# An S5 plus SwiGLU kernel: the start-up loads are shared out anew between two queues, and the first products go by halves of the contraction

## The chip, the cores and the metric

The kernel runs on one core of a Trainium2 chip. The metric is the device time of one execution in microseconds. Before the change the median of three runs is 212.19 us (211.9 to 212.24).

## The reference

The input x is 2048 rows of 512 numbers (bfloat16). Each row is normalised, and the result is the sum of x, a state-space branch and a gated feed-forward branch on the normalised rows:

```
x  = A_x
xn = _layernorm(x, axis=-1)

# state-space branch (512 complex states)
dt = exp(log_dt);  Lam_bar = exp(dt * Lam)
B_bar = ((Lam_bar - 1.0) / Lam)[:, None] * Bmat
Bu = einsum("bld,pd->blp", xn, B_bar)
h  = Lam_bar * h + Bu[:, t, :]          # for each t
y  = 2.0 * einsum("blp,dp->bld", hseq, Cmat).real + xn * Dskip

# gated branch, F = 1792
gate = xn @ w1;  up = xn @ w3
out  = (silu(gate) * up) @ w2

return x + y + out
```

## The kernel before

The 2048 rows are cut into four blocks of 512 (`TBLK`), and each block into four chunks of 128 rows (`CPB`). The 512 input features are four contraction tiles of 128 (`NDT`), the 1792 hidden features are 14 tiles `f` (`NFT`). Products want the normalised rows transposed, with features on the partitions: `xnT` of a block holds that. For blocks 1 to 3 a DMA does the transposing, off the start. For block 0 TensorE does it, chunk by chunk, since nothing else can run yet.

The order of every engine's instructions is the order in which the program writes them (`manual_schedule`); work of VectorE and ScalarE that is to lie under products waits in a queue of tasks which `drain` empties at a given rate. A transfer is issued by SP or by ScalarE, each in its own order. Transfers take completion semaphores in turn out of eight, so a transfer that gets a semaphore still in use waits, on its issuing engine, until the earlier transfer that holds it has landed.

The start, which the change touches, runs as follows.

- **Loads.** SP issues rows 0 to 127 of x (line 79), rows 128 to 255 (line 80), then by `load_w13(0, 4, 2)` (line 115) the first four tiles of w1 and w3, each as two halves of the contraction (tiles 0 and 1, then 2 and 3; 256 KB a half), then the next tiles, block 1 of x, the remaining w1 and w3, and so on. ScalarE issues a load of the first parameter vector (line 111), rows 256 to 511 (line 112) and the two other parameter vectors (lines 113 and 114).
- **Warm-up.** `keep_warm` (line 147) lets TensorE multiply constants while nothing is there: eight matmuls of 512 columns and five of 128, and two more of 128 columns between the transposes of chunk 0 and of chunk 1. Their results are never read.
- **Normalising.** `stats`, `aggr` and `normed` run on VectorE, `rstd_act` on ScalarE, chunk after chunk. `turn` transposes a chunk on TensorE into PSUM, a half (two tiles) at a time for chunks 0 and 1; `put` copies it into `xnT`, on ScalarE for chunks 0 and 1, on VectorE for 2 and 3.
- **First products.** `begun` is three pairs of PSUM banks, for the gate and the up product of f 0, 1 and 2. Their products start before the whole block is normalised: `ahead(w_sbs, fs, c, n, dts, joins)` multiplies for the tiles `fs` the chunks c to c + n with the contraction tiles `dts`. Chunk 1 is transposed by way of the banks of f 2, so that products of f 2 must wait until it has been copied out. The order (lines 516 to 551): transposes of chunk 0, of chunk 1 (both halves), the w1 products of f 0 to 2 with contraction tiles 0 and 1 for chunk 0, for chunk 1, then tiles 2 and 3 for both chunks at once, then w3, then chunk 2, a transpose of the parameters (line 544), and so on.
- **After the start** `glu_up(0)` goes on from f 0 to 13 with all four chunks, `ssm_in` makes the inputs of the scan, VectorE runs the scan, and `y_out` multiplies by w2 and by C and writes a chunk.

The parameters' transpose feeds `par_cols` (ScalarE, GpSimd), then r_col (line 549) and the load of ScalarE's table for silu (line 550).

Of the kernel before, what the change touches and what calls it, by code (L numbers as in the profile page):

```python
# [16 lines left out]
P = 128  # L17
# [3 lines left out]
def kernel(  # L21
# [24 lines left out]
    nc = tc.nc  # L46
# [8 lines left out]
    NDT = D // P  # L55
# [20 lines left out]
    def load_rows(c0, c1, eng):  # L76
        eng.dma_start(out=x_blk[0][:, c0:c1, :], in_=xv[:, 0, c0:c1, :])  # L77

    load_rows(0, 1, nc.sync)
    load_rows(1, 2, nc.sync)  # L80
    nc.scalar.preload_act_table_set("natural_log_exp_and_others")
    w1_sb = const.tile([P, NDT, F], BF16, name="w1_sb")
    w3_sb = const.tile([P, NDT, F], BF16, name="w3_sb")
    w2_sb = const.tile([P, NFT, D], BF16, name="w2_sb")
    w1v = B_w1.rearrange("(t p) f -> p t f", p=P)
    w3v = B_w3.rearrange("(t p) f -> p t f", p=P)

    H = NDT // 2

    def load_w13(f0, f1, parts=1):  # L90
        fs = slice(f0 * P, f1 * P)
        for w_sb, wv in ((w1_sb, w1v), (w3_sb, w3v)):
            for i in range(parts):
                ds = slice(i * NDT // parts, (i + 1) * NDT // parts)
                nc.sync.dma_start(out=w_sb[:, ds, fs], in_=wv[:, ds, fs])

    dskip_row = const.tile([P, D], BF16, name="dskip_row")
    bt = [const.tile([P, NDT, PS], BF16, name=f"bt{ri}") for ri in range(2)]
# [9 lines left out]
    def load_prm(i, src, eng):  # L108
        eng.dma_start(out=prm[i * NPT:(i + 1) * NPT, :], in_=src.rearrange("(t p) -> t p", p=P))

    load_prm(0, A_Lambda_re, nc.scalar)
    load_rows(2, CPB, nc.scalar)
    load_prm(1, A_Lambda_im, nc.scalar)
    load_prm(2, A_log_dt, nc.scalar)
    load_w13(0, 4, 2)
    load_w13(4, 8)
    nc.sync.dma_start(out=x_blk[1], in_=xv[:, 1, :, :])
    load_w13(8, NFT)
    nc.sync.dma_start(out=dskip_row, in_=A_Dskip.partition_broadcast(P))
    load_turned(bt[0], A_B_re)  # L120
# [26 lines left out]
    def keep_warm(n, width=512):  # L147
        one = nc.const_aps.tensor_like(1.0, like=ident[:, 0:1])
        for _ in range(n):
            nc.tensor.matmul(out=begun[0][0][:, :width], lhsT=one.to_broadcast([P, P]), rhs=one.to_broadcast([P, width]),  # L150
                             start=True, stop=True)

    keep_warm(8)
    keep_warm(5, P)


    mv_all = const.tile([P, NBLK * CPB, 2], FP32, name="mv_all")
# [4 lines left out]
    def stats(c):  # L162
        sums[c] = work.tile([P, 6], FP32, name="stats", bufs=4)
        nc.vector.bn_stats(out=sums[c], in_=x_blk[c // CPB][:, c % CPB, :])  # L164
# [4 lines left out]
    def rstd_act(c0, c1):  # L169
        y = rstd_all[:, c0:c1]  # L170
        nc.scalar.activation(out=y, in_=mv_all[:, c0:c1, 1], func=ACT.Ln, bias=LN_EPS)
        nc.scalar.activation(out=y, in_=y, func=ACT.Exp, scale=-0.5)
# [15 lines left out]
    def normed(c, parts=1):  # L188
        xn = work.tile([P, D], BF16, name="xn", bufs=8)
        for i in range(parts):  # L190
            ds = slice(i * D // parts, (i + 1) * D // parts)
            nc.vector.tensor_scalar(out=xn[:, ds], in0=x_blk[c // CPB][:, c % CPB, ds], scalar1=mv_all[:, c, 0:1],
                                    scalar2=rstd_all[:, c:c + 1], op0=ALU.subtract, op1=ALU.mult)
        return xn
# [54 lines left out]
    def turn(c, pxt, d0=0, d1=NDT):  # L249
        for dt in range(d0, d1):  # L250
            nc.tensor.transpose(out=pxt[:, dt - d0, :], in_=xn0[c][:, dt * P:(dt + 1) * P], identity=ident)  # L251

    def put(c, pxt, eng, d0=0, d1=NDT):
        dst = xnTs[0][:, d0:d1, c * P:(c + 1) * P]
        if eng is nc.scalar:
            nc.scalar.activation(out=dst, in_=pxt, func=ACT.Copy)
        else:
            nc.vector.tensor_copy(out=dst, in_=pxt)
# [110 lines left out]
    def glu_mm(b, f, w_sb, ps, ts, dts=range(NDT), joins=False):  # L369

        for dt in dts:
            nc.tensor.matmul(out=ps[:, ts], lhsT=w_sb[:, dt, f * P:(f + 1) * P], rhs=xnTs[b][:, dt, ts],  # L372
                             start=(dt == 0 and not joins), stop=(dt == NDT - 1))
# [128 lines left out]
    def ahead(w_sbs, fs, c, n=1, dts=range(NDT), joins=False):  # L502
        for f in fs:
            for w_sb in w_sbs:
                glu_mm(0, f, w_sb, begun[f][w_sb is w3_sb], slice(c * P, (c + n) * P), dts, joins)
# [13 lines left out]
    xn0[1] = normed(1, 2)  # L519
    turn(0, tb, H, NDT)  # L520
    put(0, tb, nc.scalar, H, NDT)
    keep_warm(2, P)
    turn(1, t1[0], 0, H)
    put(1, t1[0], nc.scalar, 0, H)
    turn(1, t1[1], H, NDT)
    put(1, t1[1], nc.scalar, H, NDT)
    stats(2)
    aggr(2)
    rstd_act(2, 3)
    stats(3)  # L530
    B3 = (0, 1, 2)
    lo, hi = range(H), range(H, NDT)
    ahead((w1_sb,), B3, 0, 1, lo)
    ahead((w1_sb,), B3, 1, 1, lo, True)
    ahead((w1_sb,), B3, 0, 2, hi)
    xn0[2] = normed(2)
    aggr(3)
    rstd_act(3, 4)
    ahead((w3_sb,), B3, 0, 2, lo)
    turn(2, t2)  # L540
    put(2, t2, nc.vector)
    xn0[3] = normed(3)
    ahead((w3_sb,), B3, 0, 2, hi)
    nc.tensor.transpose(out=pprm, in_=prm, identity=ident)  # L544
# [63 lines left out]
```

## Time and profile before

| | |
|---|---|
| median of three runs | 212.19 us |
| profiled execution | 212.11 us |
| its span (first to last instruction) | 210.3 us |
| TensorE (PE) busy | 206.6 us, 98% of the span |
| VectorE (DVE) busy | 173.5 us, 82% |
| ScalarE (ACT) busy | 93.4 us, 44% |
| GpSimd (POOL) busy | 6.0 us, 3% |

The span is counted from the program's first instruction to its last; 1.8 us of the execution's time lie around it. All moments in the text are microseconds from the start of the span. In a profile line `L372` is line 372 of the kernel printed above, `PE` is TensorE's multiplying, `PEld` its weight loads, `SPq` and `ACTq` the issue of transfers on SP and ScalarE. A line of the timeline has the start, the time from the first of its instructions to the end of the last, the engine, the line, the operation with the tiles written and read, their shapes and the number of instructions; in brackets is how long the engine stood idle before it and what it waited for. Matmuls overlap, so that their rate is the distance between two starts and not the time of one.

The largest groups by busy time are all products: those of w1 (58.2 us), of w3 (58.4), of w2 (51.2), of C (30.4) and of B (28.1).

### The profile page before, as it was taken

The page shows a single profiled execution, that of the slowest core. Times are in us where ns is not written, and L with a number is a line of the kernel's source. Part 1 is how long each engine was busy: PE and PEld are TensorE (multiplying, and loading weights), DVE is VectorE, ACT ScalarE, POOL GpSimd, SP SyncE. Part 2 cuts the span into 40 slices and gives each one's busy share as a digit, 9 for nine tenths or more (in the row PEclk, how much of TensorE's full clock was granted, in tenths as well). Part 3 has the DMA queues.
Part 4 walks back from the last instruction along what each step waited for, and adds up shares of the span by engine and source line. Part 5 has one row for each costly group of instructions (what it writes and reads, how often), then busy time and mean ns, then how long its engine had stood idle before and what let it go on. Part 6 is the DMA issues. An engine that isn't in the chain of part 4 may idle for free.

```text
span 210.3 us, 2878 instructions
## 1 busy us (share of the span) xinstructions
PE 206.6 (98%) x1036; PEld 97.7 (46%) x1036; DVE 173.5 (82%) x346; ACT 93.4 (44%) x167; POOL 6.0 (3%) x27
## 2 busy tenths in 40 slices
PE   8999999999999999999999999999999999999994
PEld 3864444444444444444444444444444444444453
DVE  4699989989999999999999999999999999121111
ACT  3599967666666200066666600036666620000000
POOL 2010320000000000000000000000000000000000
PEclk9999999999999999999999999999999999999999
DMA  5999599944000000000004200100000000000110
GB/s 165 294 366 219 109 178 325 217 106 100 0 3 0 0 25 25 28 26 0 0 0 77 28 1 24 50 25 5 0 0 0 0 3 25 27 25 25 34 44 25
DMA packets 25014, 13.69 MB, mean 65 GB/s; under 512 B 15912, under 2 KB 25000, under 8 KB 25000
## 3 DMA queue, kind: packets, MB, share of 16 engines
q1 hardware_dynamic: 24704, 13.24, 26.1%
q10 hardware_dynamic: 296, 0.27, 0.4%
q8 instruction: 8, 0.13, 0.3%
q14 instruction: 6, 0.05, 0.1%
HBM read 7.74 MB, written 2.10 MB: 47 GB/s over the span
## 4 chain that ended last, share of the span: by engine, by line
PE 96%; DMA 2%; SPq 0%; DVE 0%; issue 0%
PE g_ps L372 23%; PE u_ps L372 23%; PE y_ps L488 23%; PE y_ps L493 13%; PE bu_ps L411 13%; DMA w_sb<-in_B_w_dram 2%; SPq L77 0%; PE xt_ps L251 0%; DVE o L498 0%; PE xt_ps L544 0%
## 5 line engine op out<-in xcount | busy, mean ns | idle before, releaser
L372 PEld LDWEIGHTS <-w_sb 128*128 128x128 bf16 x502 | 46.4, 98 | 50.6 <-DMA w_sb<-in_B_w_dram 0.6
L372 PE MATMUL g_ps<-xnT,w_sb 128*128 128x512 bf16 (+2 forms) x254 | 58.2, 354 | 0.3 <-DMA w_sb<-in_B_w_dram 0.3
L372 PE MATMUL u_ps<-xnT,w_sb 128*128 128x512 bf16 (+2 forms) x248 | 58.4, 358 | 0.0
L488 PE MATMUL y_ps<-w_sb,hgT 128*128 128x512 bf16 (+2 forms) x238 | 51.2, 366 | 0.0
L390 ACT ACTIVATE up<-u_ps 128x512 bf16<-128x512 f32 x56 | 34.0, 607 | 14.9 <-PE u_ps L372 14.9
L413 ACT ACTIVATE u<-bu_ps 128x512 bf16<-128x512 f32 x32 | 19.1, 597 | 46.3 <-PE bu_ps L411 46.3
L388 ACT ACTIVATE sl<-g_ps 128x512 bf16<-128x512 f32 x56 | 34.0, 608 | 9.9 <-PE g_ps L372 9.2
L445 DVE TENSOR_TENSOR_SCAN ab<-r_col,h,ab 128x256 bf16<-128x256 f32 x56 | 37.7, 733 | 0.2
L488 PEld LDWEIGHTS <-hgT 128*128 128x128 bf16 x238 | 22.8, 98 | 25.9
L498 DVE TENSOR_TENSOR o<-y_ps,x_blk 128x512 bf16<-128x512 f32 (+2 forms) x17 | 11.1, 654 | 24.3 <-PE y_ps L493 24.3
L493 PE MATMUL y_ps<-ct,h 128*128 128x512 bf16 (+2 forms) x136 | 30.4, 366 | 0.0
L411 PE MATMUL bu_ps<-xnT,bt 128*128 128x512 bf16 x128 | 28.1, 379 | 0.0
L397 DVE TENSOR_TENSOR hgT<-sl,up 128x512 bf16<-128x512 bf16 x56 | 22.9, 414 | 2.1 <-ACT up L390 2.1
L493 PEld LDWEIGHTS <-h 128*128 128x128 bf16 x136 | 13.0, 98 | 14.7
L411 PEld LDWEIGHTS <-bt 128*128 128x128 bf16 x128 | 12.5, 98 | 15.1
L164 DVE BATCH_NORM_STATS2 stats<-x_blk 128x6 f32<-128x512 bf16 x16 | 10.6, 675 | 2.5 <-DMA x_blk<-in_A_x_dram 2.5
L454 DVE TENSOR_TENSOR ab<-ab,tab_s 128x2048 bf16<-128x2048 bf16 x8 | 9.8, 1222 | 0.2
L450 DVE TENSOR_TENSOR ab<-ab,tab_c 128x2048 bf16<-128x2048 bf16 x8 | 9.8, 1222 | 0.1
L427 DVE TENSOR_TENSOR ab<-u,tab_x 128x2048 bf16<-128x2048 bf16 x8 | 9.7, 1219 | 0.0
L430 DVE TENSOR_TENSOR ab<-u,tab_y 128x2048 bf16<-128x2048 bf16 x8 | 9.7, 1218 | 0.0
L201 DVE TENSOR_TENSOR x_blk<-xd,x_blk 128x512 bf16<-128x512 bf16 x16 | 6.8, 426 | 0.5
L200 DVE TENSOR_TENSOR xd<-xn,dskip_row 128x512 bf16<-128x512 bf16 x16 | 6.7, 418 | 0.0
(76 smaller groups left out, 81.3 us busy)
## 6 DMA issues: line engine op xcount, KB each, us to landing
out_dram<-o SPq DMA_DIRECT2D x15, 128.0 KB, 1.7
w_sb<-in_B_w_dram SPq DMA_DIRECT2D x1, 1792.0 KB, 9.3
x_blk<-in_A_x_dram SPq DMA_DIRECT2D x3, 512.0 KB, 6.3
w_sb<-in_B_w_dram SPq DMA_DIRECT2D x2, 768.0 KB, 7.8
w_sb<-in_B_w_dram SPq DMA_DIRECT2D x4, 256.0 KB, 5.0
w_sb<-in_B_w_dram SPq DMA_DIRECT2D x2, 512.0 KB, 4.1
x_blk<-in_A_x_dram SPq DMA_DIRECT2D x2, 128.0 KB, 2.2
x_blk<-in_A_x_dram ACTq DMA_DIRECT2D x1, 256.0 KB, 4.7
```

The source lines that it names most:

```text
L164: nc.vector.bn_stats(out=sums[c], in_=x_blk[c // CPB][:, c % CPB, :])
L372: nc.tensor.matmul(out=ps[:, ts], lhsT=w_sb[:, dt, f * P:(f + 1) * P], rhs=xnTs[b][:, dt, ts], start=(dt == 0 and not joins), stop=(dt == ...
L388: nc.scalar.activation(out=sl16, in_=g_ps, func=ACT.Silu)
L390: nc.scalar.activation(out=up16, in_=u_ps, func=ACT.Copy)
L397: nc.vector.tensor_tensor(out=hg[b][:, f, :], in0=sl16, in1=up16, op=ALU.mult)
L411: nc.tensor.matmul(out=u_ps, lhsT=bt[ri][:, dt, pt * P:(pt + 1) * P], rhs=xnTs[b][:, dt, :], start=(dt == 0), stop=(dt == NDT - 1))
L413: nc.scalar.activation(out=u16[:, :, pt, ri, :], in_=u_ps.rearrange("p (s t) -> p s t", s=NSB), func=ACT.Copy)
L445: nc.vector.tensor_tensor_scan(out=a[:, pt, 2 * ri + 1, :], data0=r_b, data1=a[:, pt, 2 * ri, :], initial=init, op0=ALU.mult, op1=ALU.add)
L450: nc.vector.tensor_tensor(out=a[:, :, 0::2, :], in0=a[:, :, 1::2, :], in1=tab_b("c"), op=ALU.mult)
L488: nc.tensor.matmul(out=y_ps[:, ds], lhsT=hg[b][:, f, cl * P:(cl + 1) * P], rhs=w2_sb[:, f, ds], start=(f == 0), stop=False)
L493: nc.tensor.matmul(out=y_ps[:, ds], lhsT=h_tiles[i][:, pt, ri, h_ts], rhs=ct[ri][:, pt, ds], start=False, stop=(pt == NPT - 1 and ri == 1))
L498: nc.vector.tensor_tensor(out=o16[:, ds], in0=y_ps[:, ds], in1=x_blk[b][:, cl, ds], op=ALU.add)
```

## The change

Rows 128 to 255 are loaded by ScalarE's queue, directly ahead of rows 256 to 511. SP's queue has rows 0 to 127, then w1's first half, w1's second half, w3's first and second half of the first four tiles, then the three parameter vectors, then everything else as it was. Five 128-column warm-up matmuls become seven. The w1 products of f 0 and 1 for chunk 0 with tiles 0 and 1 are put ahead of the transposes of chunk 1's second half; then come chunk 0 with tiles 2 and 3, chunk 1 with tiles 0 and 1, chunk 1 with tiles 2 and 3, and at last f 2 with all four tiles for both chunks.

```diff
     load_rows(0, 1, nc.sync)
-    load_rows(1, 2, nc.sync)
     nc.scalar.preload_act_table_set("natural_log_exp_and_others")
+    load_rows(1, 2, nc.scalar)
...
-    def load_w13(f0, f1, parts=1):
+    def load_w(w_sb, wv, f0, f1, eng, ds=slice(0, NDT)):
         fs = slice(f0 * P, f1 * P)
-        for w_sb, wv in ((w1_sb, w1v), (w3_sb, w3v)):
-            for i in range(parts):
-                ds = slice(i * NDT // parts, (i + 1) * NDT // parts)
-                nc.sync.dma_start(out=w_sb[:, ds, fs], in_=wv[:, ds, fs])
+        eng.dma_start(out=w_sb[:, ds, fs], in_=wv[:, ds, fs])
+
+    def load_w13(f0, f1):
+        load_w(w1_sb, w1v, f0, f1, nc.sync)
+        load_w(w3_sb, w3v, f0, f1, nc.sync)
...
-    load_prm(0, A_Lambda_re, nc.scalar)
+    low, high = slice(0, H), slice(H, NDT)
+    load_w(w1_sb, w1v, 0, 4, nc.sync, low)
     load_rows(2, CPB, nc.scalar)
-    load_prm(1, A_Lambda_im, nc.scalar)
-    load_prm(2, A_log_dt, nc.scalar)
-    load_w13(0, 4, 2)
+    load_w(w1_sb, w1v, 0, 4, nc.sync, high)
+    load_w(w3_sb, w3v, 0, 4, nc.sync, low)
+    load_w(w3_sb, w3v, 0, 4, nc.sync, high)
+    load_prm(0, A_Lambda_re, nc.sync)
+    load_prm(1, A_Lambda_im, nc.sync)
+    load_prm(2, A_log_dt, nc.sync)
     load_w13(4, 8)
...
     keep_warm(8)
-    keep_warm(5, P)
+    keep_warm(7, P)
...
     put(0, tb, nc.scalar, H, NDT)
+    B3 = (0, 1, 2)
+    lo, hi = range(H), range(H, NDT)
     keep_warm(2, P)
     turn(1, t1[0], 0, H)
     put(1, t1[0], nc.scalar, 0, H)
+    ahead((w1_sb,), (0, 1), 0, 1, lo)
     turn(1, t1[1], H, NDT)
     put(1, t1[1], nc.scalar, H, NDT)
...
     stats(3)
-    B3 = (0, 1, 2)
-    lo, hi = range(H), range(H, NDT)
-    ahead((w1_sb,), B3, 0, 1, lo)
-    ahead((w1_sb,), B3, 1, 1, lo, True)
-    ahead((w1_sb,), B3, 0, 2, hi)
+    ahead((w1_sb,), (0, 1), 0, 1, hi)
+    ahead((w1_sb,), (0, 1), 1, 1, lo)
+    ahead((w1_sb,), (0, 1), 1, 1, hi)
+    ahead((w1_sb,), (2,), 0, 2)
     xn0[2] = normed(2)
```

## The prediction, made before the changed kernel was run

> **What bounds the kernel now.** I read the stretches of TensorE first. Columns: stretch and length, PE busy us (matmuls), granted clock, DMA share, GB/s.
>
> ```profile
> 7.12:7.80 0.68, 0.68 (x10) 1.00 0.56 86
> 7.80:12.30 4.50, 4.50 (x71) 1.00 1.00 324
> 12.30:24.00 11.70, 11.70 (x59) 1.00 1.06 235
> 24.00:100.00 76.00, 76.00 (x354) 1.00 0.34 75
> 100.00:200.00 100.00, 100.00 (x465) 1.00 0.07 19
> 200.00:210.30 10.30, 7.66 (x58) 1.00 0.09 29
> ```
>
> From 7.1 us to the last products TensorE never stands still, and the list of waits has none of PE after 12 us. The edit touches only the loads and products of the first 10 us, and the columns to be multiplied stay the same. So its worth is the shift of one moment, the first u_ps product: behind it PE runs without a hole. What sets that moment is in the chain of waits in order of time (start, us, what):
>
> ```profile
> 1.64 4.80 DMA w_sb<-in_B_w_dram
> 6.43 0.05 issue
> 6.48 1.51 PE g_ps L372 x18
> 7.99 0.67 PE u_ps L372 x6
> ```
>
> The load of w1's first contraction half (I call it w1-low; w1-high is the second half) is issued at 1.64 and lands at 6.43; the 18 w1 products follow and then the w3 products. The timeline shows what else stands ready:
>
> ```profile
> 5.76 0.41 PE L251 MATMUL u_ps<-ident,xn 128*128 128x128 bf16 x2
> 6.00 0.38 ACT L256 ACTIVATE xnT<-g_ps 128x256 bf16<-128x256 bf16 x1
> ...
> 6.28 0.38 ACT L256 ACTIVATE xnT<-u_ps 128x256 bf16<-128x256 bf16 x1
> 6.47 1.90 PEld L372 LDWEIGHTS <-w_sb 128*128 128x128 bf16 x24 [0.57 <-DMA w_sb<-in_B_w_dram]
> ...
> 7.83 0.83 PE L372 MATMUL u_ps<-xnT,w_sb 128*128 128x256 bf16 x6
> ...
> 8.49 0.39 PE L251 MATMUL xt_ps<-ident,xn 128*128 128x128 bf16 x4
> ```
>
> Both transposed chunks are in xnT at 5.65 to 6.66 us, when w1-low has only just landed: the weights are the later side, but only by some tenths. The first u_ps product starts at 7.83.
>
> **The change, part by part.** Rows 128 to 255 leave SP's queue, so w1-low takes their place. The timeline of SP, an issue at a time:
>
> ```profile
> 1.64 0.43 SPq L95 DMA_DIRECT2D w_sb<-in_B_w_dram  x1
> 2.11 0.47 SPq L95 DMA_DIRECT2D w_sb<-in_B_w_dram  x1
> 6.45 0.37 SPq L95 DMA_DIRECT2D w_sb<-in_B_w_dram  x1
> ```
>
> The load of rows 128 to 255 was issued at 1.17 (chain of waits), so w1-low goes from 1.64 to 1.17 and w1-high from 2.11 to 1.64: 0.47 us earlier each. If landing moves with issue, w1-low (4.80 us in the chain) lands at 5.96. In the trace w1-high landed at 7.11, and the first product that needs it followed at 7.16; the landing becomes 6.64. Both halves of w3 move too, by 0.5 us or more (the second half is issued at 3.40 behind a wait for rows 128 to 255, which it no longer has), and were in time already.
>
> Does landing move with issue? The bytes that must come before w1-low is complete stay 768 KB (rows 0 to 511 and w1-low itself), on the same 16 DMA engines. They moved 245 GB/s in 2 to 3 us, 132 in 3 to 4 and 355 to 381 in 4 to 6: between 3 and 4 us the engines were not full, so the start is limited by issue and start-up, and I take 0.47. The lower bound is 0 (bytes decide), the upper 1.17: a 512 KB weight load lands 4.1 us after issue, at 5.27 from 1.17.
>
> The Trainium skill (DMA: Bandwidth & Descriptors, "Issuing engines are not separate DMA queues") says that queues of several engines run on the same 16 DMA engines, so that a second queue saves only issue time. By it alone, with the engines taken as full, the shift would be 0 and the sum +0.43 us; the 132 GB/s of 3 to 4 us speak against full engines, the 355 and more of 4 to 6 for them.
>
> Now the new order on PE. Before, both halves of chunk 1 (rows 128 to 255) were transposed before any product, and 12 products of w1-low, 0.67 us, covered the time until w1-high. Now only four products (w1-low, chunk 0, f 0 and 1) stand between, then the transposes of the second half of chunk 1, then products that need w1-high, first thing. So w1-high, not w1-low, decides. Behind PE's new wait for w1-low stand those transposes, behind them ScalarE's copy into xnT. By rows:
>
> - four products from 6.01. PE is still at half speed then: 128-column matmuls are 0.107 us apart up to 5.9 us (keep_warm at 5.33 and 5.43) and 0.056 from 6.48. 4 x 0.107 = 0.43, to 6.44;
> - two transposes to 6.55, visible some 0.2 later, at 6.75; ScalarE copies 0.38: 7.16, PE sees it at 7.20;
> - meanwhile w1-high (6.64, PE at 6.69): eight 128-column products (chunk 0 high, chunk 1 low), 8 x 0.056 = 0.45: 7.14, then a wait of 0.06 for the copy;
> - four products of chunk 1 high 0.22: 7.42; f 2, four of 256 columns at 0.109: 7.86.
>
> 7.86 against 7.83: +0.03 us. With a shift of 0: w1-high at 7.11, the copy seen at 7.52, then 0.23 + 0.44 and a hand-over: 8.26, +0.43. With w1 in SBUF early: products from 5.70 (copy of chunk 0), cold to 6.13, transposes to 6.34, copy seen at 7.02, 7.02 + 0.22 + 0.44 = 7.68: -0.15.
>
> The rest. Two more keep_warm matmuls: 2 x 0.107 = 0.21, from 4.66 to 4.87, where PE idled until the transpose at 4.88 waiting for xn: hidden; 0.21 us if xn were ready at once. Splitting eight products in 128 columns instead of 256: 8 x 0.056 against 4 x 0.109, 0.01.
> Rows 128 to 255 on ScalarE's queue share the engines with rows 0 to 127. Stats on rows 0 to 127 waited 1.96 us for them until 2.89; bounds 0 and 0.5 (as late as rows 128 to 255 landed, 3.38). I take 0.2: the copy of chunk 0 then comes at 5.85 instead of 5.65, still ahead of w1-low at 5.96. At 0.5 the four products begin at 6.2: 8.0, +0.17 us. Rows 256 to 511 (issue 1.53) gain about 0.2 to 0.3 us of issue; the transposes at 8.49 have xn since 8.1, so a delay of up to 0.35 us is covered.
> The three parameter loads leave ScalarE's queue (0.55, 0.38 and 0.27 us of issue, nothing waits) and come behind w3 on SP's. By the order of the changed kernel the third waits for w1-low's semaphore, and all later weights, x_blk 1, dskip and the transposed loads queue behind it. Before, the next weight load stood behind the same landing (issue at 6.45); now it follows the third parameter load: 5.96 + 0.27, still earlier. Its data are used at 14.06 us, having landed at 10.6. The parameters are transposed by PE at 9.37; the third is issued near 6.0, and other first transfers here land 2.0 to 2.2 us after issue, behind 0.5 to 1.5 of w3 data: 8.0 to 9.0, hidden by 0.3 to 1.3 us. The worst row is this load itself, which before took 3.7 us (issue 2.89, landed 6.63) beside full queues: 9.7, 0.3 late. I take hidden.
>
> Sum: 212.11 (profiled execution; span 210.3 and 1.8 around it) + 0.03 = 212.14. The three runs' median is 212.19, 0.08 above: 212.2.
>
> **The rivals.**
> Early weights. The transfers were latency-bound, w1 lands near 5.3 and 5.9, and PE comes to full speed before 5.7. For it: 132 GB/s at 3 to 4 us. Against: nothing before 6.48 ran at full speed. -0.15 as above; with 0.056 a product and transpose, ScalarE's copies (the last at 6.74) decide: 6.74 + 0.22 + 0.44 = 7.40, -0.43. 211.75 to 212.05; I name 211.85.
> Bytes decide (slower). The shift is nil because the engines carry the same 768 KB, and w1-high decides alone: +0.43, 212.6; with a late third parameter on top up to +0.7. It decides as soon as w1-high lands after 6.68. For it: from 4 us the engines move 355 GB/s and more, so w1-low's own bytes come out of a full queue.
> Clock later (slower). PE's step to full speed, now between 5.9 and 6.48, comes t later; everything from 6.5 on then loses t/2. From rows t lies between 0 and 5.7 us (0.76 to 6.48, the spell that it took); the middle gives 1.4 us, 213.6. Against: PE is busy more of the time before 6.5, not less.
> The Trainium skill (TensorE: Matmul & The Clock Gate, "Part 1: The HAM clock gate") has the speed decided once per window of about 3.4 us; a missed window would cost an estimated 1.7 us by it. The step from 0.107 to 0.056 agrees with the page; no row here shows a missed window.
> Parameters late. The third lands after 9.4 and PE stands: 0.3 to 1 us, 212.5 to 213.2.
>
> **How the numbers follow.** About 0.2% (0.42 us) is what a measurement of this kernel can tell from no change. Forecast 0.34, its own range 211.8 to 212.6; early weights 0.30, of which 0.22 beyond 0.2%, since the floor of -0.43 lies on the bound and a clock step earlier still would add to it; bytes decide 0.24, of which 0.18 beyond; clock 0.05; parameters 0.07. With 0.03 of the forecast beyond the bound on each side: faster 0.25, slower 0.33, same 0.42. The range leaves out a late clock and gains beyond 0.6: 211.6 to 213.0.
>
> **What would show it.** Right: SP issues w1-low near 1.2, it lands near 6.0, four g_ps products and then two transposes follow, a second wait of PE for w_sb near 6.4 to 6.7, the first u_ps product within 0.2 of 7.86, no wait at the prm transpose. Wrong: w1-high landing after 6.9 or before 6.2, a DVE start well after 3.1, matmuls 0.107 apart after 6.6, a prm wait, or any PE hole behind the first u_ps product.

## The result, and the profile after

The changed kernel takes 212.06 us (median of 22 runs, 211.84 to 212.36); the kernel before, run beside it, takes 211.74 us (22 runs, 211.57 to 212.34). The ratio is 1.0015, 95% interval 1.0009 to 1.0021: 0.3 us slower, between 0.2 and 0.45. It is small, but outside the noise.

The profiled execution of the changed kernel took 212.09 us with a span of 210.3, the same span as before. The 22 runs of the kernel before explain that: only three of them were as slow as the 212.11 us of the profile that the prediction worked from, and two of these three are among the three runs that it had; most lay between 211.6 and 211.8. That profile showed one of the later starts.

The chain of waits of the changed kernel in order of time (start, us, what):

```profile
1.64 5.02 DMA w_sb<-in_B_w_dram
6.66 0.04 issue
6.71 1.28 PE g_ps L377 x16
7.99 0.66 PE u_ps L377 x6
```

The transfer in the chain is now w1-high, issued at 1.64 and landed at 6.66. The timeline of the changed kernel between 2.5 and 8 us:

```profile
3.19 0.69 DVE L169 BATCH_NORM_STATS2 stats<-x_blk 128x6 f32<-128x512 bf16 x1 [2.26 <-DMA x_blk<-in_A_x_dram]
...
4.02 0.66 DVE L169 BATCH_NORM_STATS2 stats<-x_blk 128x6 f32<-128x512 bf16 x1
...
4.81 1.19 DVE L197 TENSOR_SCALAR xn<-x_blk,mv_all,rstd_all 128x256 bf16<-128x256 bf16 x4
...
5.94 0.38 PE L377 MATMUL g_ps<-xnT,w_sb 128*128 128x128 bf16 x4
...
6.16 0.28 PE L256 MATMUL u_ps<-ident,xn 128*128 128x128 bf16 x2
...
6.47 0.38 ACT L261 ACTIVATE xnT<-u_ps 128x256 bf16<-128x256 bf16 x1
...
6.71 1.28 PE L377 MATMUL g_ps<-xnT,w_sb 128*128 128x128 bf16 x16 [0.27 <-DMA w_sb<-in_B_w_dram]
...
7.83 0.38 PE L377 MATMUL u_ps<-xnT,w_sb 128*128 128x256 bf16 x2
```

The same two steps in the profile before:

```profile
2.89 0.69 DVE L164 BATCH_NORM_STATS2 stats<-x_blk 128x6 f32<-128x512 bf16 x1 [1.96 <-DMA x_blk<-in_A_x_dram]
...
4.51 1.19 DVE L192 TENSOR_SCALAR xn<-x_blk,mv_all,rstd_all 128x256 bf16<-128x256 bf16 x4
```

Four things are to be seen. The statistics of rows 0 to 127 start at 3.19, and were at 2.89 before. The normalization (TENSOR_SCALAR into xn) comes only after the statistics of the first and of the second chunk, in the order in which the program writes them: 4.81, before 4.51. PE's last wait in this execution, 0.27 us, is for w1-high and not for the rows, so that this profile alone can't tell which of the two costs the time. And the first u_ps product is at 7.83, as before; behind it PE has no hole, as these stretches show (stretch and length, PE busy us, clock, DMA share, GB/s):

```profile
7.80:12.30 4.50, 4.50 (x71) 1.00 0.91 297
12.30:24.00 11.70, 11.70 (x59) 1.00 1.10 224
24.00:100.00 76.00, 76.00 (x354) 1.00 0.29 76
```

The time of an execution minus the moment of its first u_ps product is 204.28 us in the profile before and 204.26 in the one after; in the first nine experiments below (e1 to e9) it lies between 204.26 and 204.28. So a run's time tells the moment: a median of 211.74 means 7.47, and 212.06 means 7.79. The profile before, with 7.83, is 0.36 us later than that. In it w1-low landed at 6.43; in three other profiles with the same loads (e2, e4 and e7 below) it landed at 5.50 to 5.63. The trace records sixteen completion signals for this load: in the profile before, fifteen had come by 5.67, and only the last came at 6.43.

### The profile page after: what moved, and what is told of

Its sections match the earlier page's. It is cut to its first block, busy times and chain, and to the rows that moved or that the text cites. A ratio compares the mean times of both kernels' runs of the same rounds, so it can differ in the third digit from the quotient of the medians.

```text
span 210.3 us, 2886 instructions
## 1 busy us (share of the span) xinstructions
PE 206.4 (98%) x1040; PEld 97.6 (46%) x1040; DVE 173.5 (82%) x346; ACT 93.5 (44%) x167; POOL 6.0 (3%) x27
## 4 chain that ended last, share of the span: by engine, by line
PE 96%; DMA 2%; SPq 0%; DVE 0%; issue 0%
PE u_ps L377 23%; PE g_ps L377 23%; PE y_ps L493 23%; PE y_ps L498 13%; PE bu_ps L416 13%; DMA w_sb<-in_B_w_dram 2%; PE xt_ps L256 0%; SPq L92 0%; SPq L77 0%; DVE o L503 0%; PE xt_ps L551 0%
## 5 line engine op out<-in xcount | busy, mean ns | idle before, releaser
L377 PE MATMUL g_ps<-xnT,w_sb 128*128 128x512 bf16 (+1 forms) x256 | 58.4, 353 | 0.3 <-DMA w_sb<-in_B_w_dram 0.3
```

## The experiments

All kernels below were timed against the kernel before in runs on the same chip; its median there was 211.67 us for e1 to e4, 211.79 for e5 to e8, 211.71 for e9 to e11 and 211.72 for e12. Times given are medians; the ratios are estimated from all runs and can differ a little from that of two medians. R is the theory that the rows come late, O that the order of the products costs.

**New loads alone** (`e1_loads_only`): the changed kernel with the old products and five warm-up matmuls.

```diff
-    keep_warm(7, P)
+    keep_warm(5, P)
...
-    ahead((w1_sb,), (0, 1), 0, 1, lo)
...
-    ahead((w1_sb,), (0, 1), 0, 1, hi)
-    ahead((w1_sb,), (0, 1), 1, 1, lo)
-    ahead((w1_sb,), (0, 1), 1, 1, hi)
-    ahead((w1_sb,), (2,), 0, 2)
+    B3 = (0, 1, 2)
+    lo, hi = range(H), range(H, NDT)
+    ahead((w1_sb,), B3, 0, 1, lo)
+    ahead((w1_sb,), B3, 1, 1, lo, True)
+    ahead((w1_sb,), B3, 0, 2, hi)
```

> The loads of the changed kernel (rows 128 to 255 and then 256 to 511 on ScalarE's queue, all weights and then the parameters on SP's), with the products and the warm-up of the kernel before. Theory R (rows): the 0.32 us come from rows 0 to 127 arriving 0.3 us later because rows 128 to 255 are fetched beside them; then this kernel has the loss as well: +0.2 to +0.4 us, its first statistics on VectorE start near 3.2 instead of 2.9. Theory O (order): the loss comes from the new order of the products, where PE meets the second half of w1 after four products; then this kernel loses nothing: -0.3 to +0.1 us.

212.04 against 211.67 us, ratio 1.0016 (1.0007 to 1.0024): the whole loss is there, with the old order. In its profile PE waits for the normalised rows and never for weights:

```profile
3.04 0.69 DVE L169 BATCH_NORM_STATS2 stats<-x_blk 128x6 f32<-128x512 bf16 x1 [2.11 <-DMA x_blk<-in_A_x_dram]
...
4.66 1.19 DVE L197 TENSOR_SCALAR xn<-x_blk,mv_all,rstd_all 128x256 bf16<-128x256 bf16 x4
...
7.68 0.82 PE L377 MATMUL u_ps<-xnT,w_sb 128*128 128x256 bf16 x6
```

**New order alone** (`e2_order_only`): the reverse, the old loads and warm-up with the new products.

> The new order of the products alone, with the loads and the warm-up of the kernel before. Theory R: no loss, -0.1 to +0.1 us. Theory O: +0.2 to +0.5 us, with a second wait of PE for w_sb after the first four products.

211.84, ratio 1.0008 (1.0000 to 1.0016): between the two expectations. Its profile has no wait of PE for w_sb, but this run alone doesn't decide about a small cost of the order.

**Rows 128 to 255 back on SP's queue** (`e3_rows_back`).

```diff
     load_rows(0, 1, nc.sync)
+    load_rows(1, 2, nc.sync)
     nc.scalar.preload_act_table_set("natural_log_exp_and_others")
-    load_rows(1, 2, nc.scalar)
```

> The changed kernel with rows 128 to 255 back on SP's queue, behind rows 0 to 127 and ahead of the weights. Theory R: statistics start near 2.9 again and most of the loss is gone: -0.1 to +0.1 us. Theory O: the weights are late again by 0.47 us and the order still meets them: +0.3 to +0.8 us.

212.20, ratio 1.0027 (1.0018 to 1.0037), a loss of the size that O gave. R as I had put it falls here: statistics of rows 0 to 127 start at 2.83, as R says, and yet the kernel is slower. The profiled execution, 211.85, is one of the fastest of this kernel, but its timeline has the reason in part:

```profile
2.83 0.69 DVE L169 BATCH_NORM_STATS2 stats<-x_blk 128x6 f32<-128x512 bf16 x1 [1.90 <-DMA x_blk<-in_A_x_dram]
3.90 0.69 DVE L169 BATCH_NORM_STATS2 stats<-x_blk 128x6 f32<-128x512 bf16 x1 [0.17 <-DMA x_blk<-in_A_x_dram]
```

Now the second chunk is waited for. ScalarE's queue has only rows 256 to 511 in it, which go out at 0.74 instead of 1.53 and run beside rows 128 to 255. O is settled below: e8 has the same loads with the old order and loses as much, and e9 keeps the new order and loses nothing.

**The kernel before, again** (`e4_before_again`).

> The kernel before, unchanged, for a second profile of it and as a measure of noise: within 0.1 us of its own runs. If the profile shown before was an unlucky one, its first half of w1 lands well before 6.43 here and the first product of u_ps starts well before 7.83; if it was typical, both are as before.

211.71, ratio 1.0003 (0.9994 to 1.0011). Its profiled execution has w1-low landed at 5.50, well before 6.43 as expected, but the first u_ps product only at 7.72; what held it was rows 128 to 255:

```profile
4.04 0.69 DVE L164 BATCH_NORM_STATS2 stats<-x_blk 128x6 f32<-128x512 bf16 x1 [0.39 <-DMA x_blk<-in_A_x_dram]
```

At 211.99 us this execution too is later than the median. No profile shows the kernel before at its median; the nearest with its loads is that of e7 below (211.57, first u_ps product at 7.30).

**Rows 128 to 255 behind a 1 KB load on ScalarE's queue** (`e5_rows_after_prm`): the changed kernel with these loads, and with the old products and warm-up as in e1.

```diff
-    load_rows(1, 2, nc.scalar)
...
     load_w(w1_sb, w1v, 0, 4, nc.sync, low)
+    load_prm(0, A_Lambda_re, nc.scalar)
+    load_rows(1, 2, nc.scalar)
     load_rows(2, CPB, nc.scalar)
...
-    load_prm(0, A_Lambda_re, nc.sync)
...
```

> The new loads with the old products and warm-up, but on ScalarE's queue the first parameter load (1 KB) goes ahead of rows 128 to 255, so that these are issued about 0.8 us later and rows 0 to 127 are fetched alone again. Theory R (the loss comes from two row loads at once): statistics start near 2.9 instead of 3.1, and the +0.37 us of the new loads shrinks to -0.1 to +0.15. Rival Q (the loss of the new loads lies in SP's queue, the weights or the parameters behind them): +0.3 to +0.45 us as with the new loads alone.

214.10, ratio 1.0107 (1.0086 to 1.0128): a miss by 2 us. Its timeline:

```profile
2.80 0.70 DVE L169 BATCH_NORM_STATS2 stats<-x_blk 128x6 f32<-128x512 bf16 x1 [1.87 <-DMA x_blk<-in_A_x_dram]
...
4.40 0.70 DVE L169 BATCH_NORM_STATS2 stats<-x_blk 128x6 f32<-128x512 bf16 x1 [0.69 <-DMA x_blk<-in_A_x_dram]
...
5.60 0.65 PE L256 MATMUL xt_ps<-ident,xn 128*128 128x128 bf16 x4 [0.74 <-DVE xn L197]
...
6.68 2.69 PE L377 MATMUL g_ps<-xnT,w_sb 128*128 128x128 bf16 x18
```

Rows 0 to 127 are early as R says; rows 128 to 255, issued at 1.53 beside the weights, are there only at 4.40. PE stood idle for 0.74 us before 5.60, and the 18 products that took 1.51 us in the profile before take 2.69 here: PE stayed at half speed (0.107 us from one 128-column matmul to the next) until 9.0 us. Against e7 below (211.57, the old loads), this execution loses 1.9 us: 0.8 by the late rows (first normalization at 5.23, there at 4.40), and 1.1 by the half speed (from there to the first u_ps product 3.98 us pass, there 2.90). This execution, 213.47, is one of the two fastest of the six; what the others lose beyond it is not shown.

**Five warm-up matmuls in the changed kernel** (`e6_warm5`), and **seven in the kernel before** (`e7_before_warm7`): the number in `keep_warm` alone.

> The changed kernel with five 128-column warm-up matmuls instead of seven. Theory R: the rows are late, so that the warm-up is hidden: as the changed kernel, +0.2 to +0.4 us. Theory W (warm-up): the two matmuls stand in the way of the first transposes: 0.1 to 0.2 us less than the changed kernel, +0.1 to +0.2 us.

> The kernel before with seven 128-column warm-up matmuls instead of five. In the profiled run before, PE stood idle from 4.66 to 4.88 and the two take 0.21; where rows arrive sooner than in that run they stand in the way. Theory W: +0.1 to +0.25 us; if the idle time covers them: -0.05 to +0.05 us.

212.07, ratio 1.0022 (1.0008 to 1.0036), and 211.71, ratio 0.9998 (0.9990 to 1.0007). The two matmuls show neither a cost nor a gain; W falls. The profile of e6 is a second one of the changed loads and the new order, and in it, unlike in the first, PE waits 1.10 us for the normalised rows and never for weights, with the first u_ps product at 7.84:

```profile
3.47 0.69 DVE L169 BATCH_NORM_STATS2 stats<-x_blk 128x6 f32<-128x512 bf16 x1 [2.54 <-DMA x_blk<-in_A_x_dram]
...
5.46 0.54 PE L256 MATMUL xt_ps<-ident,xn 128*128 128x128 bf16 x4 [1.10 <-DVE xn L197]
```

**Parameters on SP's queue in the kernel before** (`e8_before_prm_sp`): nothing but the three 1 KB loads is moved.

```diff
-    load_prm(0, A_Lambda_re, nc.scalar)
     load_rows(2, CPB, nc.scalar)
-    load_prm(1, A_Lambda_im, nc.scalar)
-    load_prm(2, A_log_dt, nc.scalar)
     load_w13(0, 4, 2)
+    load_prm(0, A_Lambda_re, nc.sync)
+    load_prm(1, A_Lambda_im, nc.sync)
+    load_prm(2, A_log_dt, nc.sync)
```

> The kernel before with the three parameter loads moved to SP's queue behind the first four tiles of w1 and w3; ScalarE's queue has rows 256 to 511 alone, and these are issued some 0.7 us earlier. Theory R and W: not in the way, -0.1 to +0.1 us. Rival Q: +0.15 to +0.4 us, since rows 256 to 511 now run beside rows 128 to 255 and the second half of w3 beside all, or since the parameters come late.

212.16, ratio 1.0024 (1.0012 to 1.0036), with these statistics:

```profile
3.02 0.69 DVE L164 BATCH_NORM_STATS2 stats<-x_blk 128x6 f32<-128x512 bf16 x1 [2.09 <-DMA x_blk<-in_A_x_dram]
4.13 0.69 DVE L164 BATCH_NORM_STATS2 stats<-x_blk 128x6 f32<-128x512 bf16 x1 [0.21 <-DMA x_blk<-in_A_x_dram]
```

Rival Q's number, by the first of the two causes that it named: with the 1 KB load gone from the front of ScalarE's queue, rows 256 to 511 go out at 0.74 and both row chunks that are needed first come later. The second cause, late parameters, is out: PE doesn't wait for them. e3 and e8 issue the same loads at the same moments, the one with the new order and seven warm-up matmuls, the other with the old order and five; ratios of 1.0027 and 1.0024 leave no cost of the order to be seen. Their statistics (2.83 and 3.90 against 3.02 and 4.13) show how far two single profiles of the same loads can differ. From here on the theory is R2: what counts is when both first chunks have arrived, and loads issued beside them delay them.

**The changed kernel with the row loads as before** (`e9_rows_back_late`): the third experiment with one 1 KB load in front of rows 256 to 511.

```diff
     load_rows(0, 1, nc.sync)
+    load_rows(1, 2, nc.sync)
...
-    load_rows(1, 2, nc.scalar)
...
+    load_prm(0, A_Lambda_re, nc.scalar)
     load_rows(2, CPB, nc.scalar)
...
-    load_prm(0, A_Lambda_re, nc.sync)
```

> The changed kernel with rows 128 to 255 back on SP's queue and the first parameter load (1 KB) on ScalarE's queue ahead of rows 256 to 511, which are thereby issued near 1.53 as before and not near 0.74. Theory R2 (what counts is when rows 0 to 127 and 128 to 255 have both arrived and had their statistics, and any load beside them delays them): both row loads land as before, first normalization near 4.5; 0.3 us or more faster than the same kernel without this 1 KB load in front (which lost 0.5), -0.1 to +0.2 us against before. Rival Q (parameters or weights on SP's queue, or the order): +0.3 to +0.5 us still.

211.74 against 211.71, ratio 1.0003 (0.9994 to 1.0012): the loss is gone, with the new order of products, seven warm-up matmuls, two parameters on SP's queue all still in. The timeline:

```profile
2.85 0.69 DVE L169 BATCH_NORM_STATS2 stats<-x_blk 128x6 f32<-128x512 bf16 x1 [1.93 <-DMA x_blk<-in_A_x_dram]
3.68 0.66 DVE L169 BATCH_NORM_STATS2 stats<-x_blk 128x6 f32<-128x512 bf16 x1
4.48 1.19 DVE L197 TENSOR_SCALAR xn<-x_blk,mv_all,rstd_all 128x256 bf16<-128x256 bf16 x4
...
6.25 1.28 PE L377 MATMUL g_ps<-xnT,w_sb 128*128 128x128 bf16 x16 [0.15 <-DMA w_sb<-in_B_w_dram]
...
7.37 0.82 PE L377 MATMUL u_ps<-xnT,w_sb 128*128 128x256 bf16 x6
```

Both chunks are in time, the second is not waited for, and the first u_ps product stands at 7.37. PE waits 0.15 us for w1-high.

**Rows 0 to 127 in two halves** (`e10_split`), in the kernel before: 64 rows from SP and 64 from ScalarE.

```diff
-    load_rows(0, 1, nc.sync)
+    for eng, p0 in ((nc.sync, 0), (nc.scalar, P // 2)):
+        eng.dma_start(out=x_blk[0][p0:p0 + P // 2, 0:1, :], in_=xv[p0:p0 + P // 2, 0, 0:1, :])
```

> The kernel before with rows 0 to 127 loaded as two halves of 64 rows, one issued by SP and one by ScalarE at the same moment. Theory R2: if the halves land sooner than the whole (2.7 to 2.9), everything behind them moves by as much: -0.05 to -0.25 us; if first access decides and not issue, no change, -0.05 to +0.1 us.

212.31, ratio 1.0028 (1.0018 to 1.0037): a miss. The halves take 0.58 and 0.54 us to issue, the whole took 0.40; all that follows is issued 0.2 to 0.6 us later, and the statistics start at 3.19.

**Rows 128 to 255 on ScalarE's queue, nothing else** (`e11_rows1_act`), in the kernel before.

```diff
-    load_rows(1, 2, nc.sync)
     nc.scalar.preload_act_table_set("natural_log_exp_and_others")
+    load_rows(1, 2, nc.scalar)
```

> The kernel before with one thing changed: rows 128 to 255 go first on ScalarE's queue instead of second on SP's. The parameters stay on ScalarE's queue, products and warm-up stay. Theory R2: rows 0 to 127 land at 3.0 to 3.4 instead of 2.7 to 2.9, and the time is +0.2 to +0.45 us, the whole loss of the change. Rival Q: -0.1 to +0.1 us.

213.43, ratio 1.0080 (1.0055 to 1.0105): more than either said. The profiled execution, 212.47, is the fastest of its six. Two lines of its timeline:

```profile
3.14 0.69 DVE L164 BATCH_NORM_STATS2 stats<-x_blk 128x6 f32<-128x512 bf16 x1 [2.21 <-DMA x_blk<-in_A_x_dram]
...
4.46 0.20 ACT L171 ACTIVATE rstd_all<-mv_all 128x1 f32<-128x1 f32 x1 [2.46 <-DMA w_sb<-in_B_w_dram]
```

Rows 0 to 127 are late as R2 says. In addition ScalarE stands before its first activation until w1-low has landed: by the order of this kernel its third parameter load waits for w1-low's semaphore, and the activations are queued behind it. Rows 256 to 511 land only at 6.94, and PE has a hole before their transposes at 8.85. What the slower executions lose on top, 1 us in the median, no profile shows. In the changed kernel the wait for the semaphore is on SP, where PE doesn't come to wait for what follows it; moving the parameters along with the rows avoided it.

**Rows 128 to 255 beside rows 0 to 127, rows 256 to 511 later** (`e12_rows1_prm_rows2`): the new loads with one 1 KB load between the two row loads on ScalarE's queue, old products.

> The new loads with the old products and warm-up, and the first parameter load (1 KB) on ScalarE's queue between rows 128 to 255 and rows 256 to 511: the latter are issued near 1.8 instead of 1.18, while rows 128 to 255 still go out together with rows 0 to 127. No parameter load on ScalarE's queue waits for the weights here. If the lateness comes from rows 128 to 255 beside rows 0 to 127: statistics still start at 3.0 to 3.4, +0.15 to +0.4 us. If it comes from rows 256 to 511 alone: statistics near 2.8, -0.1 to +0.1 us.

212.99, ratio 1.0048 (1.0035 to 1.0061). The statistics start at 3.30, and in e5, with the same early weights but rows 128 to 255 issued at 1.53, at 2.80: rows 128 to 255 beside rows 0 to 127 are enough to delay these. The rest are new waits: w1-high lands at 7.33 and w3's first half at 8.15, with the first u_ps product at 8.20, and rows 256 to 511 land at 7.54, their statistics start at 7.56, and PE waits for them behind the first u_ps product.

The start of the first statistics sorts the profiles (e10, with its split rows, aside). Rows 0 to 127 ahead of everything, rows 256 to 511 or rows 128 to 255 not before 1.17: 2.89, 2.93, 2.74, 2.80, 2.77, 2.85. Rows 128 to 255 at 0.74 on the other queue: 3.19, 3.04, 3.47, 3.14, 3.30. Rows 256 to 511 at 0.74 instead (e3, e8): 2.83 and 3.02, with the second chunk waited for in both. The first u_ps product follows the first normalization by 2.75 to 3.04 us in all profiles but three: 3.32 in the profile before and 3.28 in e12, where weights are late, and 3.98 in e5 at half speed.

## Why the prediction was right and where it was not

212.06 lies in the range and within 0.2% of before, as forecast. The size of the change was not forecast: +0.03 us was the sum, +0.32 was measured, on the slower side. That 212.2 as a time came so near is partly luck, since the start from which it was counted, 212.11 to 212.19, was some 0.4 us slower than the kernel before usually is, and that made up for the missing loss. By its steps:

- *The worth is the shift of the first u_ps product.* Right; the constant behind it, 204.27, held before, after and in e1 to e9.
- *w1-high at 6.64, the first u_ps product at 7.86.* 6.66 and 7.83 in the profiled execution, and the wait for w1-high came as described. The way there did not: w1-low landed at 4.92, not at 5.96, and PE never waited for it. The four products stand at 5.94 (6.01 was forecast) because they follow the transposes of chunk 1's first half at 5.80, by way of the rows. In e6, with the same loads and order, w1-high landed at 6.01, was not waited for, and the first u_ps product stands at 7.84 by way of the rows. So the agreement of the moments is in part luck.
- *The weights are the later side.* The first failed step. It was true of the one profile shown. In the repeat of the kernel before w1-low was there at 5.50, and the rows decided. In e9 PE waits 0.15 us for weights with the new order, and the time is that of the kernel before.
- *Rows 128 to 255 on ScalarE's queue: "I take 0.2 ... still ahead of w1-low at 5.96".* The step that failed: the delay, 0.30, was in its bounds, but I put its cost at nothing. w1-low, which was to hide it, had landed a microsecond before 5.96. In the profiled execution the wait for w1-high hides it instead; in e1 and e6 nothing does, and e1, without any wait for weights, has the whole loss. 0.30 is about the size of that loss. The sign named for it, a DVE start well after 3.1, is weak here (3.19) and clear in e6 (3.47). I also overlooked that rows 256 to 511, issued earlier, press on the chunks ahead of them (e3, e8), and took that earlier issue for a gain.
- *Half speed until 6.48.* Wrong for the changed kernel: its four products at 5.94 are 0.055 us apart. Over all profiles PE's step to full speed lies anywhere from 3.4 us to 9.0.
- *Parameters.* The third was issued at 4.94, landed at 8.64, and PE took it at 9.25: hidden, as said.
- *Early weights.* w1-low at 4.92 and full speed before 5.2 us were even earlier than this rival asked, but w1-high came at 6.66 instead of near 5.9, and nothing was gained. In e6, with w1-high at 6.01, the rows decided.
- *Bytes decide.* The side of the rival was right, and its cause, engines shared by both queues, fits the runs; the transfer that paid in time was not w1 but the rows. For w1-high its claim nearly held: issued 0.47 us earlier, it landed at 6.66, 6.23 and 6.01 (the changed kernel, e1, e6), against 6.38, 6.19 and 6.51 with the old loads (e2, e4, e7). What the Trainium skill says there (DMA: Bandwidth & Descriptors, "Issuing engines are not separate DMA queues") agrees with e8 and e9, where a 1 KB load in front of rows 256 to 511 is worth 0.4 to 0.5 us.
- *Clock later.* Not in the changed kernel. It happened in e5.

Of the weights, w1-low came some 0.3 to 0.7 us earlier (4.92, 5.23 and 4.89 against 5.50 to 5.63) and w1-high hardly. It was worth nothing, since in most profiles the rows set the start. How often w1-high sets it in the changed kernel is open: its own profile shows w1-high, that of e6 the rows. No version here beat the kernel before, e9 equals it. Not tried: putting the first chunk's normalization ahead of the second chunk's statistics on VectorE.

## What to carry to other kernels

Loads issued at the start on two queues are not independent: what is needed first should run alone, and a small load in front of a large one can be the spacing that protects it (e9), or make what stands behind it late (e5, e12). Before taking a start-up wait from a profile, compare the profiled time with the spread of the runs: a wait that one execution shows may be absent in most, and two executions of the same length can owe it to different waits. When a load is moved, look up which semaphore each load behind it will now wait for, and on which engine.

## What was not expected of the hardware

PE's step from half to full speed moved between profiles of nearly the same program. By the distances between the starts of its matmuls it lies near 3.4 us in e9, 3.7 in e6, between 4.9 and 5.2 in the changed kernel, between 5.9 and 6.5 in the profile before and at 9.0 in e5, while the column of the granted clock reads 1.00 in all of them. In e5 it cost about 1.1 us. Idle time alone doesn't explain that: PE waited 0.74 us there and 1.10 us in e6, which was at full speed before and after the wait. The Trainium skill (TensorE: Matmul & The Clock Gate, "Part 1: The HAM clock gate") has a free-running window of about 3.4 us in which PE must be busy. The steps of all profiles but e5, from 3.4 to 6.5 us, lie within one such window, and that the idle spell in e5, before the step, made it miss one fits too. One profile does not prove it, and e10 to e12, idle for 0.41 to 0.47 us before their steps, have them by 6.3.

Two issues of 64 rows took 0.58 and 0.54 us, one of 128 rows 0.40: half the rows are not half the issue.
